# Partitions of a half in the order (n1, a): the DRAM side of the row-reordering transfers begins with 32 instead of 2

## The chip, the core and the metric

The kernel runs on one core of a Trainium2 chip, in float32 throughout. The core has TensorE (PE; its weight loads are listed as PEld), VectorE (DVE), ScalarE (ACT), GpSimd (POOL) and SyncE (SP). Nearly all transfers are issued from SP's queue, in program order. They are carried out by 16 DMA engines. The metric is the time of one execution on the device in microseconds (us), as the median over several runs.

## What is computed

Two layers are applied in turn, twice: A, B, A, B. Each layer adds to `x`, which has 2048 rows of 512 channels, a function of the layer norm of `x`. Both use a causal convolution of length 2048 for each channel, which the reference writes with Fourier transforms of length 4096:

```python
def _A_ref(q, k, v, shift_k, ssm_k, ssm_D):
    k_pad = jnp.pad(k, ((0, 0), (ks - 1, 0), (0, 0)))
    for t in range(ks):                               # ks = 4
        k_shift = k_shift + k_pad[:, t:t + S, :] * shift_k[:, ks - 1 - t][None, None, :]
    kv = k_shift * v
    y = causal_conv(kv, ssm_k) + kv * ssm_D           # through rfft2 / irfft2, length 2 * S
    return q * y                                      # q is layernorm(x)

def _B_ref(u, log_A_real, A_imag, C_real, C_imag, log_dt, D_skip):
    dt = jnp.exp(log_dt)
    A = -jnp.exp(log_A_real) + 1j * A_imag
    C = (C_real + 1j * C_imag) * dt[:, None]
    P = jnp.exp((A * dt[:, None])[:, :, None] * pos[None, None, :])
    K = 2.0 * jnp.einsum("dn,dnl->dl", C, P).real     # 512 channels, 128 modes, 2048 taps
    return causal_conv(u, K) + u * D_skip             # u is layernorm(x)

x = A_q
for f in (A, B, A, B): x = x + f(layernorm(x), ...)
```

`causal_conv` stands for the padded transform, product and inverse transform of the reference. The convolution of layer A has the same inputs both times, since `k` and `v` do not depend on `x`; only the gate `q` differs.

## The kernel before

A row number of the 2048 is split into 32 (n1) x 2 (a) x 2 (b) x 16 (t). The arrays in DRAM lie with (a, b, n1) as 128 rows, t beside the channels, and the channels in quarters of 128 or groups of 32 (`_seq`, `_groups`, host side, unchanged). In the on-chip memory a tile has 128 partitions in two halves of 64: half b, and inside it the 64 pairs of (a, n1). The transform over those 64 positions is a matmul with the constants `w1` (forward, L179) and `w4` (backward, L362), so any order of the 64 works as long as the constants and all tiles agree.

`by_half` (L229 to L233) brings a DRAM array of 128 rows into that order: it issues two transfers from SP, one for each b, with 64 rows each. It is used for

- `kk<-ssmk_in` (L268): the long kernel of layer A, 16 groups of 32 channels
- `kvt<-kv_in` (L656): k, v and the short kernel for one of 16 groups
- `xt<-x_in` (L679): rows of x for the first layer norm's statistics
- `xr<-x_in` (L710): rows of x to be normalized, four values of t at a time, one buffer
- `out<-yo` (L923): the result, as a store.

Tiles that the kernel itself parks in DRAM between steps (`kv_d`, `ln_d`, `x1_d`, `ya_d`, `spec`) are stored and loaded as they lie, over 128 partitions. So is `kdram`, which holds the taps K of layer B: `contract` (L562 to L585) scales them into the tile `ks` with two VectorE multiplications, the second one backwards in time, in the order (b, a, t) in which they are then stored and loaded as `kk<-kdram` (L270).

The work is written out as generators. Until about 830 us two of them run interleaved by `run_steps`, one step of the first to two of the second. `stream` makes the taps of layer B (64 steps: matmuls for angles and magnitudes, exponentials, sines, products on POOL and DVE, a contraction on PE) and their spectra. `diagonal` makes the spectra of layer A's kernel (four quarters, each of four groups `kk` and eight stores `spec<-pc`), the gated products `kv` on POOL and DVE (`gated`, three steps for each of 16 groups), the row statistics, and then layer A's convolution, in which `ln_rows` normalizes x on ACT. After that follow layer B's first convolution (`conv_b(0)`), the second application of layer A, which is only a gate (`gated_update`), and `conv_b(1)`, which stores the result group by group through three buffers `yo`. A convolution runs 32 steps (four quarters of eight frequency chunks): it loads a chunk of the spectrum (`kab<-spec`, 512 KB), multiplies, and transforms back.

A scheduler arranges the instructions of each engine when the kernel is built; each engine then runs its own list in order, SP's transfers included.

Of the kernel before, what the change touches and what calls it, by code (L numbers as in the profile page):

```python
# [30 lines left out]


def dft_constants():
    n1, a, j, q = np.arange(32), np.arange(2), np.arange(32), np.arange(32)
    pos = (2 * n1[None, :] + a[:, None]).reshape(64)
    w1 = np.zeros((64, 2, 2, 32))
    w4 = np.zeros((2, 2, 32, 64))
    w2 = np.zeros((2, 2, 32, 32, 32, 2))
    mm = np.zeros((2, 32, 2, 32, 2, 2, 32))
    for k in range(32):  # L40
        for s in range(2):
            if k == 0 and s == 0:
                sign = (-1.0) ** pos
                w1[:, 0, 0, 0], w1[:, 0, 1, 0] = 1, sign
                w4[0, 0, 0], w4[0, 1, 0] = 1 / NFFT, sign / NFFT
                for i in range(32):
                    r = i // 16
                    th = 2 * np.pi * ((128 * i if r == 0 else 64 + 128 * (i - 16)) * j % NFFT) / NFFT
                    w2[0, r, :, 0, i, 0] = np.cos(th)
                    w2[0, r, :, 0, i, 1] = -np.sin(th) if i else (-1.0) ** j  # L50
                    if i == 0:
                        mm[0, 0, 0, 0, 0, 0], mm[0, 0, 1, 0, 1, 0] = 1, (-1.0) ** j
                    else:
                        mm[0, i, 0, 0, 0, r], mm[0, i, 1, 0, 0, r] = 2 * np.cos(th), -2 * np.sin(th)
                        mm[0, i, 0, 0, 1, r], mm[0, i, 1, 0, 1, r] = -2 * np.sin(th), -2 * np.cos(th)
                continue
            f = k + 64 * s if k else 32
            ang = 2 * np.pi * (f * pos % 128) / 128
            w1[:, s, 0, k], w1[:, s, 1, k] = np.cos(ang), -np.sin(ang)
            w4[s, 0, k], w4[s, 1, k] = 2 * np.cos(ang) / NFFT, -2 * np.sin(ang) / NFFT  # L60
            th = 2 * np.pi * ((f + 128 * q)[None, :] * j[:, None] % NFFT) / NFFT
            co, si = np.cos(th), np.sin(th)
            w2[s, 0, :, k, :, 0], w2[s, 0, :, k, :, 1] = co, -si
            w2[s, 1, :, k, :, 0], w2[s, 1, :, k, :, 1] = si, co
            co, si = co.T, si.T
            mm[s, :, 0, k, 0, 0], mm[s, :, 0, k, 0, 1] = co, si
            mm[s, :, 1, k, 0, 0], mm[s, :, 1, k, 0, 1] = -si, co
            mm[s, :, 0, k, 1, 0], mm[s, :, 0, k, 1, 1] = -si, co
            mm[s, :, 1, k, 1, 0], mm[s, :, 1, k, 1, 1] = -co, -si
    for c in range(1, NCH, 2):  # L70
        odd = slice(CK * c, CK * c + CK)
        mm[:, :, :, odd] = mm[::-1, :, :, odd].copy()
    w1 = w1.reshape(64, 128)
    f = lambda a: np.ascontiguousarray(a, dtype=np.float32)
    return {
        "w1": f(np.concatenate([w1, w1])),
        "w2": f(w2.reshape(128, 32, 64)),
        "mm": f(mm.reshape(128, 32, 128)),
        "w4": f(w4.reshape(128, 64)),
    }  # L80
# [24 lines left out]
def kernel(ctx: ExitStack, tc: tile.TileContext, out, x_in, kv_in, ssmk_in, ssmd_in,  # L105
                           la_in, ai_in, cr_in, ci_in, ldt_in, ldtb_in, dsk_in,
                           w1_in, w2_in, mm_in, w4_in, minus_in, tt_in, tg1_in, tg2_in, dbg=None):
    nc = tc.nc
    V, S, G, T = nc.vector, nc.scalar, nc.gpsimd, nc.tensor
# [71 lines left out]
    def fwd_group(src, z, c0, n, step, first=None, tag="c1", full=True, early=None):  # L181
        for j in range(0, n, step):
            rest = slice(0, 16)
            if early is not None:
                pf, rest = early, slice(8, 16)
            elif step == 32:
                pf = wide_bank()
            else:
                both = bank("pf", tag).rearrange("p (x n r) -> p x r n", n=32, r=2)
                pf = both.rearrange("p x r (a t) -> p a x t r", a=2)  # L190
            for i in fwd_rows(src, pf, j, step, rest, full):
                if first is not None:
                    after(i, first)
            zr = z[:, (c0 + j) // 2:(c0 + j + step) // 2].rearrange("p x k r -> p x r k")
            if step == 32:
                for r in range(2):
                    V.transpose(zr[:, :, r], pf[..., r].rearrange("p a x t -> p x a t"))
            else:
                V.transpose(zr, both)
# [27 lines left out]
        return pis, ins  # L227

    def by_half(tile_, rows, store=False):  # L229
        src = rows.rearrange("(a b n) y -> b a n y", a=2, b=2)  # L230
        for b in range(2):
            ends = tile_[64 * b:64 * b + 64], src[b]
            nc.sync.dma_start(*(ends[::-1] if store else ends))  # L233
# [27 lines left out]
    def spectrum_quarter(which, q, src, pool, zlast, zb, tag):  # L261
        z = pool.tile([128, 64, 32, 2], F32, name="zk", tag="z", bufs=zb)
        dr = pool.tile([1, 128], F32, name="dr", tag="dr", bufs=1)
        nc.sync.dma_start(dr, (ssmd_in, dsk_in)[which][:, 128 * q:128 * q + 128])
        for g in range(4):
            kk = pool.tile([128, 512], F32, name="kk", tag="kk", bufs=(NKK, 2)[which])
            if which == 0:
                by_half(kk, src[4 * q + g])  # L268
            else:
                nc.sync.dma_start(kk, src[4 * q + g])  # L270
            d = dr[:, 32 * g:32 * g + 32]
            if which == 0:
                kv = kk.rearrange("p (t c) -> p t c", c=32)
                view = lambda ps_, j, n: kv[ps_, :, j:j + n]
            else:
                kv = kk.rearrange("p (i t c) -> p t i c", i=4, c=8)
                view = lambda ps_, j, n: kv[ps_, :, j // 8:(j + n) // 8, :]
                d = d.rearrange("p (i c) -> p i c", c=8)

            G.tensor_add(kv[0:1, 0], kv[0:1, 0], d)  # L280
            fwd_group(view, z, 32 * g, 32, 16, zlast[-zb] if len(zlast) >= zb else None, tag)
            yield
        for c in range(NCH):
            if c % 2 == 0:
                pus, ins = f2_pair(z, c, None, tag)
                if c == NCH - 2:
                    zlast.append(ins)
            pu = pus[c % 2]

            if which == 1 and q == NQ - 1:  # L290
                pc = wk.tile([128, CK * 128], F32, name="pc", tag="m1", bufs=NM1)
            else:
                pc = pool.tile([128, CK * 128], F32, name="pc", tag="pc", bufs=2)
            S.copy(pc, pu.rearrange("p k c -> p (k c)"))  # L294
            nc.sync.dma_start(spec[which][q][c], pc)
            yield
# [100 lines left out]
    dt2 = gp.tile([128, NQ, 32], F32, name="dt2")  # L397
# [96 lines left out]
    rows, ms, xys, pks, angs = {}, {}, {}, {}, {}  # L494
# [67 lines left out]
    def contract(gi, k):  # L562
        xy, e2 = xys[gi, k]
        if k == 0:
            pks[gi] = pp.tile([128, 8, 64], F32, name="pk", tag="pk", bufs=1)
        pk = pks[gi]
        for i in range(2):
            for r in range(2):
                for i4 in range(4):
                    T.matmul(pk[32 * i4:32 * i4 + 32, 2 * k + i, :], e2[:, r, 4 * i + i4, :],  # L570
                             xy[:, r, 4 * i + i4, :], start=r == 0, stop=r == 1,
                             tile_position=(0, 32 * i4), skip_group_check=True)
        if k < 3:
            return
        q, g = divmod(gi, 4)
        ks = wk.tile([128, 64, 8], F32, name="ks", tag="ks", bufs=2)
        d2 = dt2[:, q, 8 * g:8 * g + 8][:, :, None, None].to_broadcast([128, 8, 2, 16])
        kv_ = ks.rearrange("p (b a t) c -> p a c b t", b=2, a=2)
        halves = lambda m0: pk[:, :, m0:m0 + 32].rearrange("p c (b t) -> p c b t", b=2)
        V.tensor_mul(kv_[:, 1], halves(0), d2)  # L580
        V.tensor_mul(kv_[:, 0, :, ::-1, ::-1], halves(32), d2)
        for i4 in range(4):
            nc.sync.dma_start(
                kdram[gi].rearrange("(s n) (i x) -> i n s x", n=32, i=4)[i4],
                ks[32 * i4:32 * i4 + 32].rearrange("p (s t) c -> p s (t c)", s=4))  # L585
# [57 lines left out]
    with ExitStack() as actx:  # L643
# [33 lines left out]
        def row_stats(t):  # L677
            xt = ap.tile([128, 512], F32, name="xt", tag="kk", bufs=NKK)
            by_half(xt, x_in[:, t, :])  # L679
            V.bn_stats(st0[:, t, :], xt)  # L680
# [345 lines left out]
```

## Time and profile before

| | us |
|---|---|
| median of 3 runs | 1158.42 (1156.01 to 1163.21) |
| the profiled execution | 1169.77 |
| its span | 1167.9 |
| PE busy in it | 669.5 |
| DVE busy | 582.7 |
| ACT busy | 412.3 |
| POOL busy | 388.7 |

The page also counts 147.43 MB of DMA traffic, 126 GB/s over the span, and a mean granted clock of TensorE of 0.738.

The views below are answers from one profiled execution. In a view of stretches each row gives a stretch, its length, the busy time of each engine (with the number of instructions), the clock granted to TensorE as a share of full speed, the mean busy share of the 16 DMA engines and their rate. A chain of waits is followed back from the last instruction: its rows give start, length and what was under way; "SPq" is the time that SP took to issue. A row of waits gives who waited at which line for what: total us, times, longest. A row of one line's instructions gives the shortest, median and longest duration in ns, the first and last start, and the shape. The page's list of transfers gives the tile, the queue, the number of issues and the size of each.

### The profile page before, as it was taken

To read this page: it belongs to the slowest core of one execution; us is meant where nothing else is said; L and a number is where in the kernel's file an instruction comes from. 1 tells how busy PE (TensorE), PEld (TensorE's weight loads), DVE (VectorE), ACT (ScalarE), POOL (GpSimd) and SP (SyncE) were. 2 spreads that over 40 slices of the span, in tenths; PEclk is the share of its full clock that TensorE was granted. 3 is DMA by queue.
4 is the path that set the end of the run, shared out by engine and by line. 5 is a ranking of instruction groups with operands and counts; after the bars stand their busy time and mean duration, and the time that the engine had idled before them with its cause. 6 is when DMAs were issued, how large, how long until landed. Compare 5 with 4: busy or idle time off the path is not lost.

```text
span 1167.9 us, 21248 instructions
## 1 busy us (share of the span) xinstructions
PE 669.5 (57%) x8648; PEld 441.8 (38%) x8648; DVE 582.7 (50%) x995; ACT 412.3 (35%) x755; POOL 388.7 (33%) x363
## 2 busy tenths in 40 slices
PE   1130332323544465885421998998765998379761
PEld 0120221212332243553311666666443665146530
DVE  3330132354544433653300785977871688977530
ACT  2100112112312232462322455554854544656310
POOL 2231142445333331432300444543341543144310
PEclk9555556655665566887655798998797899789975
DMA  4212341222122223543322465643634872245421
GB/s 141 74 66 87 116 146 68 78 78 100 67 99 84 82 96 128 160 159 99 109 72 80 140 229 167 205 147 120 210 98 163 287 257 95 89 141 203 164 98 48
DMA packets 75637, 147.43 MB, mean 126 GB/s; under 512 B 6540, under 2 KB 35732, under 8 KB 72980
## 3 DMA queue, kind: packets, MB, share of 16 engines
q1 hardware_dynamic: 74676, 143.65, 36.6%
q0 software_dynamic: 864, 2.43, 0.6%
q8 instruction: 68, 1.11, 0.4%
q14 instruction: 29, 0.24, 0.1%
HBM read 102.01 MB, written 44.04 MB: 125 GB/s over the span
## 4 chain that ended last, share of the span: by engine, by line
DMA 39%; PE 22%; SPq 12%; DVE 10%; issue 7%; ACT 6%; POOL 3%; DVEq 0%; ACTq 0%; POOLq 0%
DMA kvt<-kv_in 9%; PE pi L223 7%; SPq L233 7%; DMA spec<-pc 5%; DMA xr<-x_in 5%; DMA xt<-x_in 5%; PE pf L179 5%; PE pu L208 4%; DMA kk<-ssmk_in 4%; DMA kab<-spec 3%; PE po L362 3%; DMA u<-kv_d 3%; DMA out_dram<-yo 2%; PE pk L570 1%; PE pm L517 1%
## 5 line engine op out<-in xcount | busy, mean ns | idle before, releaser
L329 POOL TENSOR_TENSOR sw<-sw,kab 128x512 f32<-128x512 f32 x96 | 123.0, 1295 | 220.1 <-ACT sw L328 184.4
L179 PE MATMUL pf<-kk,wz 128*128 128x256 f32 x256 | 102.2, 550 | 125.4 <-DMA kk<-ssmk_in 56.3
L208 PE MATMUL pu<-zk,w 64*64 64x128 f32 x1024 | 72.2, 341 | 134.8 <-ACT pc L294 90.8
L223 PE MATMUL pi<-vv,mm 64*64 64x128 f32 x1536 | 116.0, 290 | 34.9 <-DVE vv L330 29.1
L294 ACT COPY pc<-pu 128x512 f32<-128x512 f32 x64 | 36.3, 589 | 271.9 <-DMA spec<-pc 174.2
L555 POOL TENSOR_TENSOR xy<-tt,m 128x512 f32<-128x512 f32 x64 | 88.5, 1383 | 128.0 <-ACT tt L544 67.6
L179 PEld LDWEIGHTS pf<-kk,wz 128*128 128x128 f32 x256 | 64.5, 272 | 150.8 <-issue 65.8
L330 DVE TENSOR_TENSOR vv<-pu,kab 128x512 f32<-128x512 f32 x96 | 63.0, 680 | 114.2 <-ACT sw L328 85.7
L208 PEld LDWEIGHTS pu<-zk,w 64*64 64x64 f32 x1024 | 55.5, 168 | 151.0 <-ACT pc L294 94.2
L223 PE MATMUL pi<-sw,mm 64*64 64x128 f32 x1536 | 110.9, 284 | 1.0 <-issue 1.0
L223 PEld LDWEIGHTS pi<-vv,mm 64*64 64x64 f32 x1536 | 75.7, 141 | 65.8 <-DVE vv L330 31.2
L662 DVE TENSOR_TENSOR u<-kvt 128x512 f32<-128x512 f32 x15 | 10.4, 693 | 165.9 <-DMA kvt<-kv_in 153.1
L208 PE MATMUL pu<-zu,w 64*64 64x128 f32 x1536 | 82.9, 292 | 7.8 <-DVE vv L330 4.7
L663 POOL TENSOR_TENSOR tb<-kvt 128x512 f32<-128x512 f32 x16 | 27.7, 1729 | 166.7 <-DMA kvt<-kv_in 166.7
L556 DVE TENSOR_TENSOR tt<-tt,m 128x512 f32<-128x512 f32 x64 | 66.8, 1045 | 30.6 <-ACT tt L544 30.0
L208 PEld LDWEIGHTS pu<-zu,w 64*64 64x64 f32 x1536 | 65.2, 142 | 36.6 <-DVE vv L330 14.7
L517 PE MATMUL pm<-tg,rw 64*128 64x512 f32 x96 | 48.1, 586 | 52.9 <-ACT m L519 52.9
L223 PEld LDWEIGHTS pi<-sw,mm 64*64 64x64 f32 x1536 | 77.5, 141 | 2.2 <-issue 2.2
L328 ACT COPY sw<-pu 128x512 f32<-128x512 f32 x96 | 53.4, 589 | 56.0 <-PE pu L208 55.3
L519 ACT ACTIVATE m<-pm 128x512 f32<-128x512 f32 x96 | 54.1, 598 | 52.8 <-PE pm L517 51.2
L542 ACT ACTIVATE tt<-pa 128x512 f32<-128x512 f32 x64 | 38.2, 601 | 96.1 <-PE pa L534 90.0
L570 PE MATMUL pk<-xy,tt 128*32 128x64 f32 x2048 | 53.4, 250 | 28.8 <-POOL tb L663 18.9
(143 smaller groups left out, 1265.3 us busy)
## 6 DMA issues: line engine op xcount, KB each, us to landing
kab<-spec SPq DMA_DIRECT2D x94, 512.0 KB
spec<-pc SPq DMA_DIRECT2D x64, 256.0 KB
kvt<-kv_in SPq DMA_DIRECT2D x32, 312.0 KB
kk<-ssmk_in SPq DMA_DIRECT2D x32, 128.0 KB
xr<-x_in SPq DMA_DIRECT2D x8, 512.0 KB
kv_d<-u SPq DMA_DIRECT2D x16, 256.0 KB
kdram<-ks SPq DMA_DIRECT2D x64, 64.0 KB
kk<-kdram SPq DMA_DIRECT2D x16, 256.0 KB
```

The costliest lines, as they stand in the source:

```text
L179: yield T.matmul(o, w, rhs, start=True, stop=True)
L208: ins = T.matmul(pus[odd][64 * o:64 * o + 64, i, :], w2[64 * h:64 * h + 64, k, :], z[64 * h:64 * h + 64, :, k, :], start=True, stop=True, ...
L223: ins = T.matmul(pis[odd][64 * o:64 * o + 64, i, :], mm[64 * h:64 * h + 64, k + i, 64 * part:64 * part + 64], w[part][64 * h:64 * h + 64, ...
L233: nc.sync.dma_start(*(ends[::-1] if store else ends))
L328: swapped[0] = S.copy(wb, pu)
L329: G.tensor_mul(wb, wb, kabs[s][:, 1])
L330: V.tensor_mul(wa, pu, kabs[s][:, 0])
L517: mt = T.matmul(pm, rows[gi][hs, 1, :], rhs, start=True, stop=True)
L519: i = S.activation(m, pm, AF.Exp)
L555: G.tensor_mul(xy[:, :, :, 32:64], tt[:, :, :, 1:33], m1[:, :, 32:64][:, None].to_broadcast([128, 2, 8, 32]))
L556: (G if (4 * gi + k) % E2P == E2P - 1 else V).tensor_mul(e2, e2, m2[:, None].to_broadcast([128, 2, 8, 32]))
L570: T.matmul(pk[32 * i4:32 * i4 + 32, 2 * k + i, :], e2[:, r, 4 * i + i4, :], xy[:, r, 4 * i + i4, :], start=r == 0, stop=r == 1, tile_posit ...
```

## The change

In `by_half` the dimensions of the DRAM side change places: 32 rows n outside, 2 values of a inside. Since the tile's partitions are filled in that order, the 64 partitions of a half now hold (n1, a) instead of (a, n1), and every step that depends on the order follows: the positions in `w1` and `w4` become 0 to 63, `contract` writes the taps in plain order of time, with three dimensions instead of four, and the load of `kk<-kdram` goes through `by_half` too, so it becomes two transfers of 128 KB where it was one of 256 KB. On the DRAM side a transfer had the dimensions 2, 32 and one row; now they are 32, 2 and one row. On the chip's side they are 64 partitions and one row in both kernels. PE, ACT, POOL and DVE have the same number of instructions as before, SP has 16 more transfers.

```diff
 def dft_constants():
-    n1, a, j, q = np.arange(32), np.arange(2), np.arange(32), np.arange(32)
-    pos = (2 * n1[None, :] + a[:, None]).reshape(64)
+    j, q, pos = np.arange(32), np.arange(32), np.arange(64)
...
     def by_half(tile_, rows, store=False):
-        src = rows.rearrange("(a b n) y -> b a n y", a=2, b=2)
+        src = rows.rearrange("(a b n) y -> b n a y", a=2, b=2)
         for b in range(2):
             ends = tile_[64 * b:64 * b + 64], src[b]
             nc.sync.dma_start(*(ends[::-1] if store else ends))
...
             kk = pool.tile([128, 512], F32, name="kk", tag="kk", bufs=(NKK, 2)[which])
-            if which == 0:
-                by_half(kk, src[4 * q + g])
-            else:
-                nc.sync.dma_start(kk, src[4 * q + g])
+            by_half(kk, src[4 * q + g])
...
         ks = wk.tile([128, 64, 8], F32, name="ks", tag="ks", bufs=2)
-        d2 = dt2[:, q, 8 * g:8 * g + 8][:, :, None, None].to_broadcast([128, 8, 2, 16])
-        kv_ = ks.rearrange("p (b a t) c -> p a c b t", b=2, a=2)
-        halves = lambda m0: pk[:, :, m0:m0 + 32].rearrange("p c (b t) -> p c b t", b=2)
-        V.tensor_mul(kv_[:, 1], halves(0), d2)
-        V.tensor_mul(kv_[:, 0, :, ::-1, ::-1], halves(32), d2)
+        d2 = dt2[:, q, 8 * g:8 * g + 8][:, :, None].to_broadcast([128, 8, 32])
+        kv_ = ks.rearrange("p n c -> p c n")
+        V.tensor_mul(kv_[:, :, 32:64], pk[:, :, 0:32], d2)
+        V.tensor_mul(kv_[:, :, 31::-1], pk[:, :, 32:64], d2)
         for i4 in range(4):
             nc.sync.dma_start(
                 kdram[gi].rearrange("(s n) (i x) -> i n s x", n=32, i=4)[i4],
```

## The prediction

> **What bounds the kernel now.** The page comes first: the slices by time and the chain that ended last.
>
> ```profile
> PE   1130332323544465885421998998765998379761
> PEclk9555556655665566887655798998797899789975
> DMA  4212341222122223543322465643634872245421
> DMA 39%; PE 22%; SPq 12%; DVE 10%; issue 7%; ACT 6%; POOL 3%; DVEq 0%; ACTq 0%; POOLq 0%
> ```
>
> Each digit stands for 29 us. For the first 16 slices (some 480 us) PE is busy one to four tenths, at a granted clock of about half, while the DMA engines together are busy only one to four tenths too. Yet transfers (39%) and SP's queue (12%) hold half of the chain. Something is waiting for DMA while DMA, on average, is idle. The next view, stretches of time, shows why: three short ones in which little but DMA runs, then the stages.
>
> ```profile
> core 0: us, PE busy (x) PEld busy (x) DVE busy (x) ACT busy (x) POOL busy (x), PEclk, DMA share, GB/s
> 256.00:266.00 10.00, 0.00 (x0) 0.00 (x0) 0.30 (x1) 0.00 (x0) 0.00 (x0) 0.50 0.12 47
> 1141.00:1151.00 10.00, 0.81 (x4) 0.00 (x0) 0.69 (x1) 0.00 (x0) 1.26 (x1) 0.65 0.13 51
> 836.00:845.00 9.00, 5.59 (x101) 3.85 (x99) 8.74 (x21) 6.75 (x15) 4.93 (x5) 0.88 1.00 289
> 0.00:50.00 50.00, 7.51 (x16) 5.06 (x16) 20.31 (x34) 11.46 (x17) 11.08 (x19) 0.78 0.33 113
> 0.00:480.00 480.00, 180.09 (x1438) 116.09 (x1440) 177.25 (x248) 92.62 (x156) 158.58 (x152) 0.61 0.28 96
> 480.00:650.00 170.00, 89.20 (x1015) 58.81 (x1007) 53.84 (x79) 65.29 (x109) 42.14 (x39) 0.68 0.38 117
> 650.00:800.00 150.00, 136.74 (x1975) 95.75 (x1974) 117.23 (x201) 82.14 (x146) 68.25 (x64) 0.96 0.54 173
> 840.00:990.00 150.00, 119.50 (x2082) 82.97 (x2084) 99.35 (x184) 73.25 (x150) 57.04 (x51) 0.91 0.54 184
> 1040.00:1152.00 112.00, 81.92 (x1542) 53.49 (x1540) 58.06 (x78) 38.84 (x77) 38.06 (x30) 0.89 0.45 158
> ```
>
> From 256 to 266 us only a kvt load is under way, from 1141 to 1151 us only the last output stores: the share is 0.12 and 0.13, which is 2 of 16, at 47 and 51 GB/s. In 836:845, when x<-x_d and spec<-pc move, it is 1.00 at 289 GB/s. So transfers made by by_half (line 229) use two of the sixteen DMA engines. Is that much traffic?
>
> ```profile
> kvt<-kv_in SPq DMA_DIRECT2D x32, 312.0 KB
> kk<-ssmk_in SPq DMA_DIRECT2D x32, 128.0 KB
> xr<-x_in SPq DMA_DIRECT2D x8, 512.0 KB
> kk<-kdram SPq DMA_DIRECT2D x16, 256.0 KB
> xt<-x_in SPq DMA_DIRECT2D x32, 128.0 KB
> out_dram<-yo SPq DMA_DIRECT2D x32, 128.0 KB
> ```
>
> kvt, kk<-ssmk_in and xt are 32 x 568 KB = 18.6 MB; at 49 GB/s they keep those two engines busy for 380 of the first 480 us. The outputs, 4.2 MB, take 86 us of the last 112. This is the limit, and the rest of the chain follows from it:
>
> ```profile
> by line: DMA kvt<-kv_in 22.6%; SPq L233 14.9%; DMA spec<-pc 11.8%; DMA xt<-x_in 11.3%; DMA kk<-ssmk_in 8.7%; SPq L672 2.7%; DMA u<-kv_d 2.6%; PE pf L179 2.2%; DMA kk<-kdram 2.1%; SPq L751 2.0%; DMA ai<-ai_in 1.5%; PE pu L208 1.4%; issue 1.3
> POOL tb L663 <- DMA kvt<-kv_in: 166.7, 15, 15.7
> ACT pc L294 <- DMA spec<-pc: 174.2, 19, 47.4
> 250.63 15.49 DMA kvt<-kv_in
> ```
>
> The first row is the chain from 0 to 480 us. spec<-pc, SP's issue at L233 and u<-kv_d are not slow by themselves: a store over all sixteen engines ends only when its share on the two crowded ones has passed.
>
> **The change, part by part.** The DRAM side of by_half goes from dimensions (a 2, n 32, y) to (n 32, a 2, y). The SBUF side stays 64 partitions, each row stays whole, and the number of rows is the same.
>
> *Engines per transfer.* I take it that two engines were used because the outer DRAM dimension is 2, and that 32 gives all sixteen. The trace has the two ends (0.12 and 1.00) but no transfer with this new order. At 289 GB/s the 18.6 MB take 64 us of sixteen engines, inside a stage whose share was 0.28, so DMA stops being its limit.
> By the Trainium skill ("DMA: Bandwidth & Descriptors", section on why a DMA increments its semaphore by 16), the number of engines is the largest up to 16 that divides the slowest dimension of both sides. The trace agrees for the old order (0.12 is 2/16); by that rule the new one has 16.
>
> *Stage 0 to 480.* What is late next? Engine work does not vanish: PE, DVE, ACT and POOL sum to 609 us in 480 (1.27 busy at once). The stages without by_half traffic run at 404/150 = 2.70 (650:800) and 349/150 = 2.33 (840:990). The first 50 us hold a serial set-up with 50 us of work (their row: 7.5 + 20.3 + 11.5 + 11.1), which I leave at 40 us. PE's work shrinks by some 40 us if its clock rises from 0.61 towards 0.91. So (609 - 50 - 40)/2.33 + 40 = 263 us. I choose the lower of the two rates since kv, spectrum and tap steps pass work between POOL and DVE many times. Gain 217, taken as 215. At 2.70 it is 248; at 1.94 (217/112, the rate of 1040:1152) it is 480 - 307 = 173.
>
> *Stage 480 to 650.* ln_rows loads a megabyte into one buffer, and ACT, in order, waits with the convolution's copies behind it.
>
> ```profile
> by line: DMA xr<-x_in 32.7%; DMA u<-kv_d 11.0%; DMA ln_d<-xr 6.6%; ACT xr L713 6.2%; PE pi L223 5.1%; issue 5.1%; SPq L583 5.0%; PE pf L179 4.0%; PE pm L517 2.9%; PE pu L208 2.6%; SPq L715 1.7%; ACT L543 1.5%; PE pa L529 1.3%; SPq L233 1.3%
> 528.09 3.48 DMA ln_d<-xr
> 532.33 27.85 DMA xr<-x_in
> 569.20 27.67 DMA xr<-x_in
> 615.37 18.78 DMA u<-kv_d
> ```
>
> 1.05 MB at 289 GB/s is 3.6 us; with about 3 us to land (a 256 KB ln_d store took 3.48) I take 7 us, and 5 for the u behind the last xr: 21 + 21 + 14 = 56 us, taken as 55. By concurrency (250 us of work at 2.33 is 107 us) it would be 63; if half of the next wait appears instead, 28.
>
> *Stages 650 to 1040.* No by_half traffic; PE is busy 137 of 150 us. Nothing.
>
> *Last stage.*
>
> ```profile
> 906.36 5.80 DMA kab<-spec
> 1076.08 10.87 DMA kab<-spec
> 1090.17 12.00 DMA out_dram<-yo
> 1111.56 12.90 DMA kab<-spec
> 1139.84 11.51 DMA out_dram<-yo
> ```
>
> Without stores beside it a kab load in the chain took 5.80: 5 + 7 from the two kab, 8 from the store at 1090 and 7.5 from the last one, if each lands in 4. That is 27; PE is already busy three quarters of this stage, and by concurrency its middle gives less (217/2.33 = 93, or 19 less). I take 22, bounds 12 and 30.
>
> *kk<-kdram.* Now by_half as well: 32 issues instead of 16.
>
> ```profile
> L233 SPq DMA_DIRECT2D kk<-ssmk_in x32: 503/2511/10507, 5.6 to 403.5; - x32
> L270 SPq DMA_DIRECT2D kk<-kdram x16: 319/338/1238, 272.0 to 882.2; - x16
> ```
>
> 16 x (2 x 0.50 - 0.34) = 11 us of SP over 600 us, of which SP works little; nothing to 11. [...]
> The Trainium skill speaks against this split (same page, "Rules for kernel authors": two transfers to disjoint halves serialize, use one over 128 partitions); by it the sum would be those 11 us worse.
>
> *The two multiplications into ks.* The same 256 elements per partition, three dimensions instead of four.
>
> ```profile
> L580 DVE TENSOR_TENSOR ks<-pk,dt x16: 578/618/659, 266.8 to 877.9; 128x256 f32<-128x256 f32 x16
> L581 DVE TENSOR_TENSOR ks<-pk,dt x16: 624/643/686, 267.3 to 878.3; 128x256 f32<-128x256 f32 x16
> 194.42 0.42 DVE L557 SCALAR_TENSOR_TENSOR xy<-tt,m 128x256 f32<-128x256 f32 x1
> 252.11 1.49 DVE L557 SCALAR_TENSOR_TENSOR xy<-tt,m 128x256 f32<-128x256 f32 x1
> ```
>
> 32 instructions; between the fastest and the slowest operation of that size, 0.42 and 1.49, lies -7 to +27 us of DVE, which waits in these stages. Taken as nothing. The constants (pos, w1, w4) only change values, and the instructions on PE, ACT and POOL stay the same in number and almost in order.
>
> **Sum.** 215 + 55 + 22 = 292. The profiled execution took 1169.8 us (span 1167.9), 11 above the median of 1158.4. 1169.8 - 292 = 878, and 11 lower beside the other runs: 867, given as 865.
>
> **Rivals.**
> *SP's order is the metronome.* SP is one queue in program order: a wait for ACT's pc or DVE's vv holds all loads behind it, and three kvt and kk buffers reach only so far ahead. For it: stage 480:650 manages 250/170 = 1.47, and L672 and L583 stand in the chains. Against: in those rows the cause is itself a late by_half transfer. At 1.47 the first stage is 519/1.47 + 40 = 393, a gain of 87, with 28 and 12 from the others: 1169.8 - 127 - 11 = 1032, given as 1030.
> *Slower: two engines remain, and kk<-kdram joins them.* If something else than the outer DRAM dimension (the 64 partitions, say) limits by_half, the change only moves 16 loads of 256 KB from sixteen engines (0.9 us at 289 GB/s) to two (5.35 at 49): 71 us more on the crowded pair, in a kernel whose Pool adds wait for kk<-kdram now. With 10 us of issues and half of the rest hidden it gives 1158 + 45 = 1205. It decides if the share stays at 0.12 while by_half runs alone. Against it: kk<-kdram's neighbours with 64 source rows (kab) land 512 KB in 5.80 us, which two engines cannot.
> *No change.* The order of rows as issued could be put back to the outer 2, with the new load hidden: 1158.
>
> **Chances.** Forecast 0.83, SP's order 0.10, slower 0.04, no change 0.03. The forecast's own range: gains of 173 + 28 + 12 = 213 and of 232 + 63 + 30 = 325 give 946 and 834; on the good side the set-up, which waits for loads too, may shorten, and DVE and POOL may lose their slow cases (0.42 against 1.49 us for one form), for which I allow 44; on the other side 19 for the issues and the two multiplications. So 790 to 965, which leaves out the rivals, 0.17. Faster by over 1% (about the least that a measurement of this kernel tells from no change): 0.93, within 1% 0.03, slower 0.04.
>
> **What would show it.** Right: a share above 0.5 while kvt or xr lands, kvt no longer first in the chain, L233 near 0.5 us at the median, xr waits near 7 us, the last store near 4, granted clock in the first stage above 0.75, and the first stage over before 300 us. Wrong: the same clock and share with kvt still the wait (two engines remain), or kvt landing fast while the first stage stays above 350 us, with SP's waits for ACT, POOL and DVE in its place.

## The result, and the profile after

| | before | after |
|---|---|---|
| median, us | 1159.28 (4 runs, 1156.01 to 1163.21) | 805.56 (4 runs, 793.55 to 815.95) |
| profiled execution / its span | 1169.77 / 1167.9 | 815.95 / 814.1 |
| PE, DVE, ACT, POOL busy | 669.5, 582.7, 412.3, 388.7 | 631.9, 598.3, 411.6, 391.9 |

By the medians the ratio is 0.695, 354 us less, and the profiled executions lie as far apart. The ratio on record, 0.688 (95% interval 0.681 to 0.696), is that of the fast runs alone, which after the change are the two of 802.73 and 793.55 us. The profiled execution after is the slowest of its four. The forecast of 865 was right in direction and cause, and 59 us too high; the time lies near the lower end of its range.

The engines do the same work, only closer together. First the slices of the page after (20 us each):

```profile
PE   1567656877799777999699998773799982779995
PEclk9557756778789888699989999698989996899998
DMA  8989426565834477867456444552587724047774
```

DMA starts at eight and nine tenths, and PE is no longer starved in the first quarter. Then the stretches, in the columns shown above: the set-up, the first stage as it now is (to the last row statistic), the very end with the last stores alone, and the last stage.

```profile
0.00:50.00 50.00, 19.36 (x112) 15.05 (x112) 37.04 (x45) 12.54 (x19) 33.17 (x43) 0.78 0.89 238
0.00:216.00 216.00, 140.05 (x1240) 90.84 (x1240) 178.47 (x219) 84.50 (x142) 155.42 (x143) 0.72 0.69 198
809.50:812.00 2.50, 0.00 (x0) 0.00 (x0) 0.43 (x1) 0.00 (x0) 0.00 (x0) 0.50 0.90 195
708.00:814.00 106.00, 86.88 (x1663) 56.98 (x1661) 73.60 (x110) 48.64 (x101) 43.45 (x36) 0.96 0.60 180
```

Stores that ran at a share of 0.13 now run at 0.90. In the page's list of transfers the median time from issue to landing is given after, and SP's own time for kk (shortest, median, longest in ns) has fallen from 2,511 to 548 at the median:

```profile
kvt<-kv_in SPq DMA_DIRECT2D x32, 312.0 KB, 5.6
kk<-ssmk_in SPq DMA_DIRECT2D x32, 128.0 KB, 6.0
xr<-x_in SPq DMA_DIRECT2D x8, 512.0 KB, 9.5
```

```profile
L232 SPq DMA_DIRECT2D kk<-ssmk_in x32: 528/548/2544, 5.8 to 183.9; - x32
```

In the waits of the whole execution the two DMA rows of the prediction have become small (174.2 and 166.7 us before). The longest wait is POOL for ACT, both of which are compute; it led the list before too, in the first row here, and the other rows are after:

```profile
POOL sw L329 <- ACT sw L328: 184.4, 37, 64.6
POOL sw L325 <- ACT sw L324: 154.4, 46, 17.6
ACT pc L290 <- DMA spec<-pc: 31.4, 11, 8.7
POOL tb L658 <- DMA kvt<-kv_in: 15.0, 8, 3.6
```

Three marks cut the execution into the prediction's stages: the last row statistic (the tile xt), the last normalization of xr, and the first statistics behind layer B's first convolution. The rows of those lines, first before and then after (the last two numbers ahead of the shape are the first and last start):

```profile
L680 DVE BATCH_NORM_STATS2 st<-xt x16: 680/694/697, 312.0 to 470.1; 128x6 f32<-128x512 f32 x16
L713 ACT ACTIVATE xr<-xr,nb,rs x16: 797/798/817, 520.4 to 636.3; 128x512 f32<-128x512 f32 x16
L952 DVE BATCH_NORM_STATS2 st<-x x16: 275/276/294, 993.3 to 996.2; 128x6 f32<-128x128 f32 x16
```

```profile
L675 DVE BATCH_NORM_STATS2 st<-xt x16: 643/672/695, 143.0 to 216.2; 128x6 f32<-128x512 f32 x16
L708 ACT ACTIVATE xr<-xr,nb,rs x16: 797/804/813, 279.1 to 340.5; 128x512 f32<-128x512 f32 x16
L947 DVE BATCH_NORM_STATS2 st<-x x16: 274/276/293, 678.6 to 681.5; 128x6 f32<-128x128 f32 x16
```

| stage | before, us | after, us | gained | forecast |
|---|---|---|---|---|
| to the last xt statistic | 470 | 216 | 254 | 215 |
| to the last xr | 166 | 124 | 42 | 55 |
| to the end of layer B's first convolution | 357 | 338 | 19 | 0 |
| to the end | 175 | 136 | 39 | 22 |
| sum | 1168 | 814 | 354 | 292 |

### The profile page after: what moved, and what is told of

Same layout as the page of the kernel before. It is cut to its first block, busy times and chain, and to the rows that moved or that the text cites. A ratio compares the mean times of both kernels' runs of the same rounds, so it can differ in the third digit from the quotient of the medians.

```text
span 814.1 us, 21290 instructions
## 1 busy us (share of the span) xinstructions
PE 631.9 (78%) x8648; PEld 420.4 (52%) x8648; DVE 598.3 (73%) x995; ACT 411.6 (51%) x755; POOL 391.9 (48%) x363
## 5 line engine op out<-in xcount | busy, mean ns | idle before, releaser
L178 PE MATMUL pf<-kk,wz 128*128 128x256 f32 x256 | 90.5, 498 | 48.0 <-DMA rows_d<-hl 13.8
L222 PE MATMUL pi<-vv,mm 64*64 64x128 f32 x1536 | 112.0, 286 | 18.6 <-DVE vv L326 12.2
L222 PEld LDWEIGHTS pi<-vv,mm 64*64 64x64 f32 x1536 | 71.6, 138 | 47.4 <-DVE vv L326 16.3
L178 PEld LDWEIGHTS pf<-kk,wz 128*128 128x128 f32 x256 | 57.7, 243 | 70.7 <-POOL kk L276 33.5
L207 PE MATMUL pu<-zu,w 64*64 64x128 f32 x1536 | 77.2, 283 | 8.1 <-DVE vv L326 4.0
L207 PE MATMUL pu<-zk,w 64*64 64x128 f32 x1024 | 66.3, 330 | 18.5 <-ACT pc L290 10.4
L553 DVE SCALAR_TENSOR_TENSOR xy<-tt,m 128x256 f32<-128x256 f32 x64 | 57.5, 898 | 29.2 <-ACT tt L539 18.5
L222 PEld LDWEIGHTS pi<-sw,mm 64*64 64x64 f32 x1536 | 73.3, 139 | 2.9 <-issue 2.9
L207 PEld LDWEIGHTS pu<-zk,w 64*64 64x64 f32 x1024 | 51.6, 162 | 36.5 <-ACT pc L290 12.1
L338 ACT COPY ie<-pi 128x512 f32<-128x512 f32 x64 | 34.4, 589 | 54.8 <-PE pi L222 49.3
L358 PE MATMUL po<-w,w 128*64 128x512 f32 x192 | 53.3, 643 | 8.5 <-DVE w L352 5.2
```

Of the source, the lines that this page charges most:

```text
L178: yield T.matmul(o, w, rhs, start=True, stop=True)
L207: ins = T.matmul(pus[odd][64 * o:64 * o + 64, i, :], w2[64 * h:64 * h + 64, k, :], z[64 * h:64 * h + 64, :, k, :], start=True, stop=True, ...
L222: ins = T.matmul(pis[odd][64 * o:64 * o + 64, i, :], mm[64 * h:64 * h + 64, k + i, 64 * part:64 * part + 64], w[part][64 * h:64 * h + 64, ...
L358: ins = T.matmul(po[64 * a:64 * a + 64], w4, ws[g][:, :, 16 * a:16 * a + 16, :].rearrange("p x t r -> p t x r"), start=True, stop=True, ti ...
L553: V.scalar_tensor_tensor(xy[:, 1, :, 0:32], tt[:, 1, :, 0:32], -1.0, m1[:, :, 0:32], op0=ALU.mult, op1=ALU.mult)
```

## Experiments

The theory is that the slowest dimension on the DRAM side sets the number of DMA engines. Its rival is that the gain comes from the order of the partitions, the plainer taps, or the order in which memory is read. To tell them apart the tiles keep the new order, and only the arrays in DRAM are laid out differently on the host, so that the same 64 rows are fetched with another outer dimension. The output, which is returned in the reference's shape, is put back into order on the host too.

```diff
-    def by_half(tile_, rows, store=False):
-        src = rows.rearrange("(a b n) y -> b n a y", a=2, b=2)
+    def by_half(tile_, rows, store=False, o=0):
...
+        if o:
+            src = rows.rearrange("(b w u) y -> b u w y", b=2, u=o)
+        else:
+            src = rows.rearrange("(a b n) y -> b n a y", a=2, b=2)
...
+# row b * 64 + w * o + u of an array in DRAM holds partition b * 64 + u * (64 // o) + w of its tile
+def _order(o):
+    tile_ = (64 * np.arange(2)[None, None, :] + 32 * np.arange(2)[:, None, None] + np.arange(32)[None, :, None]).reshape(2, 64)
+    return tile_.reshape(2, o, 64 // o).transpose(0, 2, 1).reshape(128)
...
+    arrays["kv_in"] = np.ascontiguousarray(arrays["kv_in"][:, _order(2)])
...
```

**Two outside again.**

> The changed kernel, its tiles in the new order (n1, a), but the input and output arrays lie in DRAM so that the transfers of kvt, kk<-ssmk_in, xt, xr and the output begin with a dimension of 2 (2, 32, row) in place of 32; kk<-kdram stays at 32. Engines theory (the outer DRAM dimension sets how many DMA engines a transfer gets): two engines again, DMA share 0.12 to 0.13 while only such a transfer runs, time 1140 to 1180. Rival, order (the gain is from the order of the partitions, the plainer taps or the order in which rows are fetched): near 806.

Measured: 1159.01 us, ratio to the kernel before 0.995 (0.992 to 0.999). The whole gain is gone, with the new order of the partitions and the new taps in place, so these two do not make it. The order in which memory is read is not settled by this run: with 2 outside the inner rows now lie two apart in DRAM, which neither kernel has. The quarters further down settle it.

**Four, eight, sixteen.**

> The same with a dimension of 4 outside (4, 16, row). Engines theory: four engines, share 0.25 when alone. The 18.6 MB of the first stage take 190 us of four engines; with about 88 us of other traffic on each engine (share 0.28 of 480 us is 134, less 46 that the crowded two add to the mean) the four are busy 278 us, so the first stage takes some 285 us instead of 216, the xr waits and the stores add 10 to 25 us: 880 to 920. Rival, order: near 806. A rule of all or nothing (anything under 16 falls back to two): near 1158.

> The same with a dimension of 8 outside (8, 8, row). Engines theory: eight engines; 95 + 88 = 183 us of the first stage, less than the 216 it takes by its engines' work, so it is nearly hidden: 800 to 840. All or nothing: near 1158.

> The changed kernel with the same five transfers at (16, 4, row) instead of (32, 2, row). If the number of engines is the outer dimension up to the sixteen that there are: the same as the changed kernel, 795 to 815, share near 1 when alone. If 32 rows outside gave more than the number of engines (shorter chains on each engine, say): between 815 and the 835 of the eight.

Measured: 927.03 us with four (ratio 0.796, 0.791 to 0.801), 835.11 with eight (0.718, 0.714 to 0.722), 803.50 with sixteen (0.691, 0.686 to 0.695). Four is a little slower than the 880 to 920 expected, the times of the others are as expected. The share while only the last stores move is read from stretches near the end, here with two, four and eight outside:

```profile
1144.00:1152.00 8.00, 0.00 (x0) 0.00 (x0) 0.00 (x0) 0.00 (x0) 0.00 (x0) 0.50 0.13 51
```

```profile
913.00:923.00 10.00, 0.00 (x0) 0.00 (x0) 0.69 (x1) 0.00 (x0) 0.00 (x0) 0.71 0.26 82
```

```profile
824.00:828.00 4.00, 0.00 (x0) 0.00 (x0) 0.69 (x1) 0.00 (x0) 0.00 (x0) 1.00 0.49 159
```

0.13, 0.26, 0.49 and, with 32 outside, 0.90 above: 2, 4, 8 and nearly 16 of 16 engines. So 2 is no special case, and from 16 to 32 nothing more is won. One expectation was missed: with sixteen outside the last stores alone show 0.61 (796 to 799 us, at 202 GB/s), not a share near 1. That is still more than nine engines, and between 6 and 16 us, when SP issues mostly kk and kvt, the share of that run is 0.98 at 293 GB/s. Its median times from issue to landing are also those of the change: 5.8 us for kvt, 7.8 for xr and 3.6 for the stores, against 5.6, 9.5 and 3.8. Why the share of the last stores differs (0.61 and 0.90 at about the same rate) was not tried.
This is the rule of the Trainium skill ("DMA: Bandwidth & Descriptors", section on why a DMA increments its semaphore by 16), and the runs agree with it, by the share at 2, 4, 8 and 32, and at 16 by the time and the landing.

**The old order, in quarters.**

```diff
         src = rows.rearrange("(a b n) y -> b a n y", a=2, b=2)
         for b in range(2):
-            ends = tile_[64 * b:64 * b + 64], src[b]
-            nc.sync.dma_start(*(ends[::-1] if store else ends))
+            for a in range(2):
+                ends = tile_[64 * b + 32 * a:64 * b + 32 * a + 32], src[b, a]
+                nc.sync.dma_start(*(ends[::-1] if store else ends))
```

> The kernel before, with its old order (a, n1) and its old taps, but each by_half is four transfers of 32 rows (32, row) instead of two of (2, 32, row). Engines theory: sixteen engines without the new order, so almost the whole gain, less what 136 more issues of 0.53 us (72 us of SP) put on the path: 806 to 850. Rival, order: near 1158 or above by the issues.

Measured: 801.16 us, ratio 0.690 (0.686 to 0.694). The kernel before reaches the time of the changed one with no new order at all, and with each half read in the same order of rows as before, which rules out the rest of the rival. The 136 further issues cost nothing that can be measured.

**One family at a time.** Each of the next kernels is the changed one with a single family at 2 outside; all else stays at 32. For kvt, with `by_half` and `_order` as above:

```diff
-            by_half(kvt.rearrange("p t c -> p (t c)"), kv_in[grp])
+            by_half(kvt.rearrange("p t c -> p (t c)"), kv_in[grp], o=2)
...
+    arrays["kv_in"] = np.ascontiguousarray(arrays["kv_in"][:, _order(2)])
```

> The changed kernel with kvt alone put back to a dimension of 2 outside (by the layout of kv_in in DRAM). If the crowding of two engines over the first stage is the cost: 10.2 MB at 49 GB/s are 208 us, with 88 us of other traffic 296 us against the 216 that the stage now takes: 870 to 900. If kvt's own landing time were the whole of it (three buffers ahead, 12 us a group, 16 groups = 192 us): below 216 us, so near 806.

> The changed kernel with xr alone at 2 outside (through a second copy of x_in, laid out for it). The prediction's term for this stage: 55 us more, 850 to 870. If the late xr was mostly the queueing behind kvt, kk and xt on the two engines: 10 to 25 us more.

> The changed kernel with the output stores alone at 2 outside. The prediction's term: 22 us more, 820 to 835. The two traces, from the second gate to the end 145 us before and 106 after: 39 us more, 840 to 850.

> The changed kernel with kk<-ssmk_in alone at 2 outside: 4.2 MB at 49 GB/s are 86 us, with 88 us of other traffic 174 us on the two engines in a stage of 216: hidden, 803 to 820. If a spectrum's load is on the path for itself (32 halves of 2.7 us instead of some 0.5): up to 860.

> The changed kernel with xt alone at 2 outside (second copy of x_in). The same 86 us, but all in the last 80 us of the first stage, where the two engines then have too much to do: 820 to 845. If hidden like kk: 803 to 820.

| family on two engines | us | more than 805.56 | expected |
|---|---|---|---|
| kvt | 951.28 | 146 | 64 to 94 |
| xr | 883.95 | 78 | 44 to 64 |
| out | 856.94 | 51 | 14 to 44 |
| kk<-ssmk_in | 855.31 | 50 | 0 to 14, or up to 54 |
| xt | 852.66 | 47 | 14 to 39 |
| sum | | 372 | |

They ran in several sessions, in which the median of the kernel before lay between 1159 and 1170 us, so a difference is good to some 10 us. The row of kk is the least sure: three of its runs took 855 to 857 us and one 841.36, which would be 36 us. The sum, 372, is near the 354 that separate the two kernels: the families hardly cover for each other. The traces, cut by the same three marks, put the losses where the families run: 140 us (kvt), 40 (kk) and 46 (xt) ahead of the last xt statistic, 59 (xr) from there to the last xr, 40 (out) in the last stage.

All but kk lie above every case of their expectations. For kk the case that held is the second, a load that is on the path for itself: PE waited 32.6 us for it, against 4.0 after. The added-up load of the two engines was too small a measure for kvt and xt as well; a likely reason, not tested, is that it supposes that the two engines are always fed, while SP issues in program order and in bursts. What a slow family does is seen in the waits of the first stage, with kvt on two engines and then with kk on two:

```profile
POOL tb L664 <- DMA kvt<-kv_in: 147.2, 14, 15.0
ACT pc L296 <- DMA spec<-pc: 96.1, 12, 18.5
```

```profile
ACT pc L296 <- DMA spec<-pc: 53.8, 9, 24.8
PE pf L178 <- DMA kk<-ssmk_in: 32.6, 4, 19.6
POOL tb L664 <- DMA kvt<-kv_in: 32.6, 9, 7.1
```

In the second fence kvt and spec<-pc run on all sixteen engines, yet their waits are 32.6 and 53.8 us where the same stage after has 15.0 and 29.9. So a family on two engines costs the families beside it too. Whether their transfers land later or only start later is open: these traces have no times of landing, and the longest single issue of a kvt load also grew, from 1.8 to 5.2 us of SP.

**The taps on two engines.** The kernel before, with kk<-kdram through its old by_half and the new multiplications:

```diff
-            if which == 0:
-                by_half(kk, src[4 * q + g])
-            else:
-                nc.sync.dma_start(kk, src[4 * q + g])
+            by_half(kk, src[4 * q + g])
...
```

> The kernel before, its old order and two engines, but kk<-kdram loaded by halves on the two engines too, with the new multiplications into ks: the case of the prediction's slower rival. Its price: 10 us of issues and half of 71 us on the path, 1190 to 1220. If the loads of the taps come at times when the two engines are free: 1158 to 1170.

Measured: 1205.27 us, ratio 1.037 (1.031 to 1.042). Pool's wait for these loads grew from 62.3 to 98.8 us:

```profile
POOL kk L277 <- DMA kk<-kdram: 98.8, 14, 20.7
```

So the prediction's slower rival was priced rightly (1205); only its condition did not hold. That half of the 71 us would be hidden was an assumption; the growth of Pool's wait, 36.5 us, is near the other half.

**Whole tiles.** The arrays lie in DRAM in the order of the tiles, and each by_half of kvt, kk<-ssmk_in, xt, xr and out is one transfer over 128 partitions (taps as in the change).

```diff
+        if o == 1:
+            nc.sync.dma_start(*((rows, tile_) if store else (tile_, rows)))
+            return
...
+    arrays["kv_in"] = np.ascontiguousarray(arrays["kv_in"][:, _order(1)])
...
```

> The changed kernel with kv_in, ssmk_in, x_in and the output laid out in DRAM in the order of the tiles, so that each by_half of them is one transfer over 128 partitions: 68 transfers fewer. If SP's issue time is now on the path: 68 x 0.53 = 36 us of SP less, up to 20 us faster, 785 to 800. If it is hidden: 800 to 810.

Measured: 815.15 us, ratio 0.697 (0.693 to 0.701): not faster than the change (0.681 to 0.696), and above both cases of the expectation. So less issuing by SP brings no gain now. By the three marks this version wins 19 us from the last statistic to the last xr (105 against 124) and loses 18 from there to the end of layer B's first convolution (356 against 338), a stretch that holds none of the transfers that differ; why it is longer there was not tried.
The Trainium skill (same page, "Rules for kernel authors") advises one transfer over 128 partitions in place of two halves; no run here shows a gain from that.

No version among the runs is measurably faster than the change; with sixteen outside and the old order in quarters it is equalled.

## Why the prediction was right, point by point

- **Two engines, by the outer dimension.** Shown: the dose of 2, 4, 8, 16 and 32 with its shares and times, and the old order in quarters.
- **The range.** Its lower sum has a slip: it adds 232, which is the length of the first stage at the rate of 2.70, where the gain, 248, belongs. With 248 it is 818 instead of 834, and the measured 806 lies below both. So the time is inside the range by the 44 us allowed beyond the sum. Of the two reasons given for them one fits what came, a set-up that overlaps with other work; the other did not come, since the DVE form whose slow cases were to go (xy<-tt,m, L557 before) has a mean of 898 ns after and had 777 before.
- **First stage: 215 forecast, 254 measured.** The mechanism held, two choices in its sum were too careful. The rate: 2.33 busy engines at once was chosen, 2.70 named as the other end. The row from 0 to 216 us has 140 + 178 + 85 + 155 = 558 us of work in 216, or 2.59 over all of it, with DVE busy 83%. The set-up: 40 us were set apart as serial, but the first 50 us now hold 102 us of work instead of 50, because the groups of kvt and kk run beside it. PE was to lose 40 us with a faster clock. To the same mark it lost 31 (171 to 140), some 9 of them only because 83 of its 1323 matmuls now come behind the mark; its granted clock rose from 0.60 to 0.72, not above the 0.75 named.
- **xr: 55 forecast, 42 measured in its stage.** From the first to the last xr it is 115.9 against 61.4, or 54.5, the term as it was worked out; 13 us are given back between the last statistic and the first xr, where some of the work moved behind the first mark has to be done. The load lands in 9.5 us at the median instead of 7. With xr alone on two engines the kernel loses 78 us, of which 17 are in the first stage (its last statistic starts at 233.3 instead of 216.2), where the first xr is loaded early, and 59 in its own.
- **Last stage: 22 forecast, 39 measured.** This term was mis-sized. It was priced from the two kab and two store pieces of the chain, 27 us, and then cut since PE was three quarters busy. With the stores alone on two engines the loss is 51 us, 40 of them in this stage (176 against 136), and in that run's waits stand rows that are nearly gone after (there 3.9 and 7.7 us, and 2.2 for the store):

```profile
POOL sw L331 <- DMA kab<-spec: 36.8, 12, 9.1
DVE vv L332 <- DMA kab<-spec: 27.9, 13, 7.0
DVE yo L922 <- DMA out_dram<-yo: 16.1, 4, 6.8
```

  So more kab loads were late than the two that the chain named: 12 and 13 waits here. The prediction had a figure that points to it: 86 us of stores on the two engines in 112.
- **640 to 990 us: nothing forecast, 19 measured.** Not from the two engines: with two outside the same stretch (last xr at 647.5, first statistics at 982.4) takes 335 us, even less than the 338 after. The kernels with the old order take 347 to 364 us for it and those with the new one 329 to 356, so the order may have a part in it; what makes these 19 us was not tried.
- **Split of kk<-kdram, multiplications: nothing.** Right as far as it can be seen. The quarters keep the whole load and the old multiplications and take the same time as the change; the multiplications have the same means, 621 and 650 ns before, 617 and 649 after.
- **SP's order as the metronome (1030).** It fell: SP's waits for compute remain, the first stage runs at 2.59 all the same.

## What to carry to other kernels

Look at the DMA share while one transfer runs alone: a steady 2, 4 or 8 of 16 was its outer dimension here, and the average share of the page (0.28 in the first stage) hid the bottleneck. Make the outer dimension on the DRAM side 16 or 32, by the order of the partitions, by the layout in DRAM, or by splitting the transfer; here all three gave the same time. With a family of transfers on few engines the waits for the well-spread ones beside it grew too, so its price is higher than its own waits.

## What was not expected of the hardware

The number of issues on SP's queue hardly mattered. The five families took 272 issues of 0.42 us at the median in quarters (some 114 us of SP), 136 of 0.55 in the change (75) and 68 of 0.34 as whole tiles (23); the times were 801.16, 805.56 and 815.15 us. And eight of sixteen engines were nearly enough, 835 against 806 us, though the DMA share of the first stage is 0.69 with all sixteen.
